# Banded attention with a ratio MLP: the attention's split matmuls replaced by plain float32 in quarter and half tiles of the array

## The chip, the cores and the metric

One core of one Trainium2 chip. The time is device microseconds of one execution. Before: 1083.75 us, median of 3 runs (1083.62 to 1083.78).

## The reference

Eight sequences of 576 positions, eight heads of 64. Each query sees the 128 keys up to its own; the result goes through an MLP whose activation is a ratio of polynomials.

```python
scores = scale * np.matmul(q, k.transpose(0, 1, 3, 2))
mask = (rel >= 0) & (rel < 128)
scores = np.where(mask, scores + bias[None], -1000000000.0)
attn = softmax(scores)                       # with 1e-9 in the denominator
x = (attn @ v).transpose(0, 2, 1, 3).reshape(B * S, H * D)    # 4608 x 512
h = x @ w_in                                 # 4608 x 2048
g = (a0 + a1 h + a2 h^2 + a3 h^3) / (1 + |b0| |h| + |b1| h^2 + 1e-6)
out = g @ w_out                              # 4608 x 512
```

All inputs and the output are float32.

## The kernel before

The 4608 tokens are 36 blocks of 128. The MLP takes them in 17 tiles t: 3 blocks, then 15 times 2, then 3 (`MLP`, L32). Attention works in units: a pair p of heads (128 rows: two heads of 64) and one or two blocks j (`TILES`, L30). A block of queries needs its own block of keys and the one before, 256 keys; a block at which a sequence begins (`kinds` 1) needs its own alone. While the MLP of tile t runs, the units of tile t + 1 are worked off.

For matmuls the kernel has two ways. In tile 0 operands are plain float32. From tile 1 on each operand is split into a high part of type float32r and the rest, and a product is three float32r matmuls: high by high, high by low, low by high. The weights are split once (`split`, L562), the keys, queries and values at every load.

A unit of `attention` (L400), with the lines that the change touches:

- `job` (L354) loads kqv into one buffer `kqv_raw`, ACT casts keys with queries and values to the high part (L389), DVE subtracts for the low part (L390).
- `scores` (L427): for each block and each of the three products, one matmul per head with 64 rows, 128 query columns as weights and 256 keys streaming (L433); head 0 is in rows 0 to 63, head 1 in rows 64 to 127, each with its own accumulator sc0, sc1.
- L447 copies, under the mask id_sb, the scores of the block before over those of the own block where a key lies ahead of its query, so that each query keeps 128 scores. L453 adds the bias and takes the top, L458 (ACT) the exponential with its sum, L466 to L468 the normalization.
- L477 transposes the probabilities on PE into pt; ACT (L480) and DVE (L482) make the high and low part p_all.
- POOL selects (L488, L489) the part that belongs to the own keys into p_own and leaves the rest in p_all, both with high and low.
- `values` (L495): for each block, own keys and then keys before, three matmuls of 128 rows, 128 value columns (both heads) and 256 streaming columns (both heads' probabilities, L500). Of the result px only the two diagonal head parts are used. Each of these up to four groups is a step of its own.
- ACT (L516) copies px into x_hi and DVE (L518) subtracts for x_lo, once per head over 64 partitions.

The MLP's matmuls are L599 (up, into h) and L655 (down, into acc), with the activation between on ACT, DVE and POOL. In tile 0 the weights arrive as 64-bit floats seen as two 32-bit words and are converted on POOL, ACT and DVE (`convert`, L529).

The order of everything is made ahead by a planner (`Plan`, L76): each step has a due time, engines and an estimated cost; the planner walks through time, gives each engine the earliest due step whose inputs and buffers are ready, and the instructions are written in that order, one fixed queue per engine. The constants at L265 to L271 are due times and offsets. Nothing is reordered at run time except by waits.

Of the kernel before, what the change touches and what calls it, by code (L numbers as in the profile page):

```python
# [20 lines left out]
P = 128  # L21
# [231 lines left out]
def banded_attention_ratio_mlp(ctx: ExitStack, tc: tile.TileContext, kqv, w_in, w_out, ab, bias, ident, out):  # L253
    nc = tc.nc
    const = ctx.enter_context(tc.tile_pool(name="const", bufs=1))
    sb3 = ctx.enter_context(tc.tile_pool(name="sb3", bufs=3))
# [3 lines left out]
    count = {id(const): 1, id(ps1): 1, id(sb2): 2, id(sb3): 3, id(ps3): 3}  # L260
    eng = {"p": nc.tensor, "a": nc.scalar, "v": nc.vector, "g": nc.gpsimd, "s": nc.sync}
    NTILE = len(MLP)


    A0, DA, T0, L0, L1 = -3.5, 1.542, 22.056, 90.639, 24.589  # L265
    AOFF, D2, D3, JL, VL = -0.627, 3.694, 6.675, 9.175, 4.671
    SP, SV, SA, SG = 0.204, 0.035, 0.013, 0.218
    LL = -1.886
    ML, ZA, ME, OE = 23.116, 0.956, 0.92, 12.957
    C0, DC, CO, DO, WL = 2.237, 6.361, 21.961, 5.327, 5.885  # L270
    S0, DS, SL, AW, BL = 120.646, 2.26, 6.993, 24.311, 4.541  # L271
# [82 lines left out]
    def job(u):  # L354
# [8 lines left out]
        if t == 0 and j == 0:  # L363
            plan.op(u0 - JL, {"s": 364}, lambda e: eng[e].dma_start(ap(first_kq)[:, p], src[:, P : 3 * P]), writes=[(first_kq, p)])
            plan.op(u0 - JL + VL, {"s": 182}, lambda e: eng[e].dma_start(ap(first_v)[:, p], src[:, 4 * P :]), writes=[(first_v, p)])
            kt = lambda part, b0, b1: ap(first_kq)[:, p, (b0 - 1) * P : (b1 - 1) * P]
            qt = lambda part, i: ap(first_kq)[:, p, P : 2 * P]
            vt = lambda part, b: ap(first_v)[:, p]
            return kt, qt, vt, 1, [(first_kq, p)], [(first_v, p)]
        if t == 0:  # L370
            tag = "hi" if p % 2 == 0 else "lo"
            kq = slot(sb2, [P, KMAX + QMAX], F32, "kq_32", tag="kq_" + tag)
            v = slot(sb2, [P, KMAX], F32, "v_32", tag="v_" + tag)
            plan.op(u0 - JL, {"s": 728 * 5 / 4}, lambda e: eng[e].dma_start(ap(kq), src[:, : W - ks]), writes=[(kq, 0)])
            plan.op(u0 - JL + VL, {"s": 546}, lambda e: eng[e].dma_start(ap(v), src[:, W - ks :]), writes=[(v, 0)])
            kt = lambda part, b0, b1: ap(kq)[:, b0 * P : b1 * P]
            qt = lambda part, i: ap(kq)[:, ks + i * P : ks + (i + 1) * P]
            vt = lambda part, b: ap(v)[:, b * P : (b + 1) * P]
            return kt, qt, vt, 1, [(kq, 0)], [(v, 0)]
        kq_hi = slot(sb2, [P, KMAX + QMAX], F32R, "kq_hi")  # L380
        kq_lo = slot(sb2, [P, KMAX + QMAX], F32R, "kq_lo")
        v_hi = slot(sb2, [P, KMAX], F32R, "v_hi")
        v_lo = slot(sb2, [P, KMAX], F32R, "v_lo")
        raw = slot(const, [P, WMAX], F32, "kqv_raw", tag="raw")
        plan.op(u0 - JL, {"s": 2002 * W / 1408}, lambda e: eng[e].dma_start(ap(raw)[:, :W], src), writes=[(raw, 0), (raw, 1)], after=1000 * (u0 - AW))
        for n, (c0, c1) in enumerate(((0, W - ks), (W - ks, W))):
            hi, lo = (kq_hi, kq_lo) if n == 0 else (v_hi, v_lo)
            N = c1 - c0
            plan.op(u0 - 4 + 2 * n, {"a": act(N, 0)}, lambda e, hi=hi, N=N, c0=c0, c1=c1: nc.scalar.copy(ap(hi)[:, :N], ap(raw)[:, c0:c1]), reads=[(raw, n)], writes=[(hi, 0)])  # L389
            plan.op(u0 - 3 + 2 * n, {"v": dve(N)}, lambda e, hi=hi, lo=lo, N=N, c0=c0, c1=c1: nc.vector.tensor_tensor(ap(lo)[:, :N], ap(raw)[:, c0:c1], ap(hi)[:, :N].bitcast(F32), ALU.subtract),  # L390
                    reads=[(raw, n), (hi, 0)], writes=[(lo, 0)], sb=True)
        kt = lambda part, b0, b1: ap((kq_hi, kq_lo)[part])[:, b0 * P : b1 * P]
        qt = lambda part, i: ap((kq_hi, kq_lo)[part])[:, ks + i * P : ks + (i + 1) * P]
        vt = lambda part, b: ap((v_hi, v_lo)[part])[:, b * P : (b + 1) * P]
        return kt, qt, vt, 2, [(kq_hi, 0), (kq_lo, 0)], [(v_hi, 0), (v_lo, 0)]
# [4 lines left out]
    def attention(u):  # L400
# [3 lines left out]
        kt, qt, vt, parts, kq_keys, v_keys = job(u)  # L404
# [14 lines left out]
        if t == 0 and u % 2:  # L419
            sc = [slot(ps1, [P, 2, 2, P], F32, f"sc{h}", tag=f"acc{h}") for h in range(2)]  # L420
        else:
            sc = [slot(ps1, [P, 2, 2, P], F32, f"sc{h}", tag=f"sc{h}") for h in range(2)]
# [4 lines left out]
        def scores(e, i):  # L427
            seq = ((0, 0), (0, 1), (1, 0)) if parts == 2 else ((0, 0),)
            b0 = i + own_only[i]
            for n, (x, y) in enumerate(seq):  # L430
                for h in range(2):
                    r = slice(64 * h, 64 * h + 64)
                    nc.tensor.matmul(ap(sc[h])[:, i, own_only[i] :], qt(x, i)[r], kt(y, b0, i + 2)[r], start=(n == 0), stop=(n == len(seq) - 1))  # L433

        def all_scores(e):
            for i in range(m):
                scores(e, i)

        o1 = plan.op(A, {"p": 187 + 354 * m if parts == 2 else sum(430 if x else 860 for x in own_only)}, all_scores, reads=kq_keys, writes=[(sc[0], 0), (sc[1], 0)], rows=0.5)
# [30 lines left out]

        pt = slot(ps1, [P, 4 * P], F32, "pt", tag="ptx")
        dt = F32R if parts == 2 else F32
        w = slot(sb2, [P, parts, 4 * P], dt, "p_all")

        def transpose(e):
            for y in range(n):
                nc.tensor.transpose(ap(pt)[:, y * P : (y + 1) * P], ap(pr)[:, y, :], ap(id_sb)[:, 0])  # L477

        o2 = plan.op(A + D2, {"p": 28 + 108 * n}, transpose, reads=[(pr, y) for y in range(n)] + [(id_sb, 0)], writes=[(pt, 0)])
        plan.op(A + D2 + 0.2, {"a": act(n * P, 1)}, lambda e: nc.scalar.copy(ap(w)[:, 0, : n * P], ap(pt)[:, : n * P]), reads=[(pt, 0)], writes=[(w, 0)])  # L480
        if parts == 2:
            plan.op(A + D2 + 0.3, {"v": dve(n * P)}, lambda e: nc.vector.tensor_sub(ap(w)[:, 1, : n * P], ap(pt)[:, : n * P], ap(w)[:, 0, : n * P].bitcast(F32)), reads=[(pt, 0), (w, 0)], writes=[(w, 1)])  # L482
        own = w
        if blocks:
            own = slot(const, [P, parts, 4 * P], dt, "p_own")
            pick = lambda y: ap(y)[:, :, : n * P].rearrange("p a (y q) -> p a y q", q=P)
            cost = {"g": 135 + 0.93 * parts * n * P}
            plan.op(A + D2 + 0.5, cost, lambda e: nc.gpsimd.affine_select(out=pick(own), in_=pick(w), pattern=[[0, parts], [0, n], [1, P]], compare_op=ALU.is_ge, fill=0.0, base=0, channel_multiplier=-1), reads=[(w, 0), (w, 1)], writes=[(own, 0), (own, 1)])  # L488
            plan.op(A + D2 + 0.6, cost, lambda e: nc.gpsimd.affine_select(out=pick(w), in_=pick(w), pattern=[[0, parts], [0, n], [-1, P]], compare_op=ALU.is_ge, fill=0.0, base=-1, channel_multiplier=1), reads=[(w, 0), (w, 1)], writes=[(w, 0), (w, 1)])  # L489
        if t not in xs:  # L490
            xs[t] = [slot(sb2, [P, NKC, P * MLP[t]], F32 if t == 0 else F32R, "x_hi"), slot(const, [P, NKC, P * MLP[t]], F32R, "x_lo", tag=f"x_lo{t % 2}") if t else None]
        xh, xl = xs[t]
        px = slot(ps3, [P, 4 * P], F32, "px", tag="h") if t == 0 else slot(ps1, [P, 4 * P], F32, "px", tag="ptx")

        def values(e, i, half, first, last):  # L495
            y = own if half else w
            c = slice(2 * i * P, 2 * (i + 1) * P)
            seq = ((0, 0), (0, 1), (1, 0)) if parts == 2 else ((0, 0),)
# [260 lines left out]
```

## Time and profile before

| | |
|---|---|
| median of 3 runs | 1083.75 us |
| the profiled execution | 1083.98 us, span 1082.2 us |
| DVE_READ and ACT reads of accumulators (L453, L458) | 23.7 and 54.3 us |
| DMA read and written | 58.07 MB and 9.44 MB, 62 GB/s over the span |

Read first the busy shares, then the stages: the attention of tile 0 and the load and conversion of the weights fill the first 120 us, splitting the weights the time to about 240 us, and from there every MLP tile of two blocks repeats with four attention units in it. A row of the table of stages has the stretch, its length, the busy time of PE, of its weight loads (PEld), DVE, ACT and POOL, each with a count of instructions, then PE's granted clock, the DMA engines' busy share and GB/s. PE's matmuls overlap in the records, so the time that one occupies PE is read from start to start.

### The profile page before, as it was taken

Reading aid. Unit: us, or ns where it says so; the run is one execution under the profiler, and the core shown is the slowest. Engines: PE = TensorE matmul, PEld = TensorE weight load, DVE = VectorE, ACT = ScalarE, POOL = GpSimd, SP = SyncE. Lnnn points to the kernel's source line nnn. Section 1 sums busy time; section 2 is a strip of 40 time slices with the busy share of each in tenths; the row PEclk is TensorE's granted clock in tenths of the full one; section 3 lists DMA queues with packets and bytes.
Section 4 is the critical chain, followed back from the end, with each engine's and each line's share of the span. In section 5 each row is a group of like instructions: output and inputs, shape, how many; then the busy total and the mean of one; then the engine's idle time right before and its main releaser. Section 6 shows DMA issues by size and latency. Waiting matters only on the chain.

```text
span 1082.2 us, 19767 instructions
## 1 busy us (share of the span) xinstructions
PE 1053.0 (97%) x6827; PEld 902.0 (83%) x6827; DVE 948.6 (88%) x2190; ACT 774.1 (72%) x1786; POOL 589.3 (54%) x581
## 2 busy tenths in 40 slices
PE   6899899999999999999999999999999999999998
PEld 4555468899889898989899989989899989888897
DVE  5899899998989898989988889989898989899776
ACT  6766778776767686867776777777676767677664
POOL 3745489854555464546455545555454545546442
PEclk9999999999999999999999999999999999999999
DMA  9625511020201111111111020111110202011000
GB/s 306 202 76 164 151 61 40 26 78 25 79 25 63 46 65 44 60 43 65 42 37 62 28 82 28 63 39 60 44 65 20 80 30 76 21 59 39 20 1 30
DMA packets 35477, 68.79 MB, mean 64 GB/s; under 512 B 3376, under 2 KB 19632, under 8 KB 35376
## 3 DMA queue, kind: packets, MB, share of 16 engines
q1 hardware_dynamic: 35376, 67.52, 19.1%
q8 instruction: 54, 0.88, 0.3%
q14 instruction: 47, 0.39, 0.1%
HBM read 58.07 MB, written 9.44 MB: 62 GB/s over the span
## 4 chain that ended last, share of the span: by engine, by line
PE 82%; DVE 7%; POOL 3%; ACT 3%; DMA 2%; issue 2%; SPq 0%; DVEq 0%; ACTq 0%; POOLq 0%
PE h L599 34%; PE acc L655 33%; PE px L500 8%; PE sc L433 5%; PE pt L477 2%; DMA raw_w<-in_w_out 1%; POOL pr L468 1%; DVE h L632 1%; POOL w_lo L574 1%; DVE g_p L626 1%; ACT pr L458 1%; DVE cv L558 1%; DVE g_p L627 1%; DVE v_lo L390 1%; DVE w L559 1%
## 5 line engine op out<-in xcount | busy, mean ns | idle before, releaser
L599 PE MATMUL h<-x_hi,wi_hi 128*128 128x256 f32 (+1 forms) x1024 | 302.5, 295 | 1.2 <-DVE g_l L640 1.2
L599 PE MATMUL h<-x_lo,wi_hi 128*128 128x256 f32 (+1 forms) x1024 | 291.0, 284 | 0.0
L623 POOL TENSOR_SCALAR g_q<-g_u,babs 128x512 f32<-128x512 f32 (+1 forms) x152 | 116.3, 765 | 307.6 <-ACT g_u L622 292.5
L599 PE MATMUL h<-x_hi,w_lo 128*128 128x256 f32 (+1 forms) x960 | 274.0, 285 | 1.5 <-DVE w_lo L574 1.5
L599 PEld LDWEIGHTS h<-x_lo,wi_hi 128*128 128x128 f32 x1024 | 192.5, 188 | 31.9 <-issue 0.7
L599 PEld LDWEIGHTS h<-x_hi,wi_hi 128*128 128x128 f32 x1024 | 192.6, 188 | 28.2 <-DVE g_l L640 1.8
L655 PE MATMUL acc<-wo_hi,g_h 128*128 128x512 f32 x528 | 209.0, 396 | 0.0
L625 POOL TENSOR_TENSOR g_q<-g_q,g_u 128x512 f32<-128x512 f32 (+1 forms) x152 | 191.0, 1257 | 8.9
L655 PE MATMUL acc<-w_lo,g_h 128*128 128x512 f32 x495 | 194.7, 393 | 0.0
L655 PE MATMUL acc<-wo_hi,g_l 128*128 128x512 f32 x528 | 194.3, 394 | 0.3 <-DVE g_l L640 0.3
L599 PEld LDWEIGHTS h<-x_hi,w_lo 128*128 128x128 f32 x960 | 180.6, 188 | 2.4 <-DVE w_lo L574 1.7
L622 ACT ACTIVATE g_u<-h 128x512 f32<-128x512 f32 (+1 forms) x152 | 87.0, 572 | 101.5 <-PE h L599 99.5
L628 ACT ACTIVATE g_u<-g_q,guard 128x512 f32<-128x512 f32 (+1 forms) x152 | 106.5, 701 | 50.3 <-POOL g_q L625 49.5
L488 POOL TENSOR_SCALAR_AFFINE_SELECT p_own<-p_all 128x1024 fp32r<-128x1024 f32 (+1 forms) x72 | 78.1, 1085 | 89.3 <-DVE p_all L482 88.7
L626 DVE TENSOR_TENSOR g_p<-h,g_p 128x512 f32<-128x512 f32 (+1 forms) x152 | 100.3, 660 | 29.9 <-ACT g_p L624 28.4
L458 ACT ACTIVATE pr<-pr,st 128x128 f32<-128x128 f32 x288 | 112.6, 392 | 18.2 <-DVE st L453 17.4
L631 DVE SCALAR_TENSOR_TENSOR g_q<-g_q,h 128x512 f32<-128x512 f32 (+1 forms) x152 | 99.6, 655 | 29.1 <-ACT h L630 25.4
L624 ACT ACTIVATE g_p<-h,na 128x512 f32<-128x512 f32 (+1 forms) x152 | 114.6, 754 | 0.5 <-DVE h L632 0.2
L640 DVE TENSOR_TENSOR g_l<-h,g_h 128x512 fp32r<-128x512 f32 (+1 forms) x136 | 90.9, 669 | 24.3 <-ACT g_h L639 23.4
L632 DVE SCALAR_TENSOR_TENSOR h<-g_p,na,h 128x512 f32<-128x512 f32 (+1 forms) x152 | 109.5, 720 | 0.1
L627 DVE SCALAR_TENSOR_TENSOR g_p<-g_p,na,h 128x512 f32<-128x512 f32 (+1 forms) x152 | 108.2, 712 | 0.6
L639 ACT CAST g_h<-h 128x512 fp32r<-128x512 f32 (+1 forms) x136 | 77.8, 572 | 40.7 <-DVE h L638 40.3
(91 smaller groups left out, 2257.5 us busy)
## 6 DMA issues: line engine op xcount, KB each, us to landing
kqv_raw<-in_kqv SPq DMA_DIRECT2D x64, 512.0 KB, 3.4
out<-o SPq DMA_DIRECT2D x33, 256.0 KB, 2.4
raw_w<-in_w_in SPq DMA_DIRECT2D x16, 512.0 KB, 4.4
raw_w<-in_w_out SPq DMA_DIRECT2D x16, 512.0 KB, 4.7
bias_t<-in_bias SPq DMA_DIRECT2D x44, 64.0 KB, 1.8
kq<-in_kqv SPq DMA_DIRECT2D x4, 320.0 KB, 5.6
kqv_raw<-in_kqv SPq DMA_DIRECT2D x4, 320.0 KB, 3.5
v<-in_kqv SPq DMA_DIRECT2D x4, 192.0 KB, 5.9
```

What stands on the lines that cost most here:

```text
L458: nc.scalar.activation(ap(pr)[:, y, :], ap(pr)[:, y, :], AF.Exp, bias=ap(st)[:, y : y + 1], scale=-1.0, accum_out=ap(st)[:, 4 + y : 5 + y])
L599: nc.tensor.matmul(h(n), w[:, k, :], x[:, k, :], start=(k == 0 and m == 0), stop=(k == NKC - 1 and m == len(seq) - 1))
L623: plan.op(E, {"g": tsc}, lambda e: nc.gpsimd.tensor_scalar(v(g_q), v(g_u), ap(babs)[:, 1:2], ap(babs)[:, 0:1], ALU.mult, ALU.add), reads=[ ...
L624: plan.op(E, {"a": act(W, 1, 2) - 20}, lambda e: nc.scalar.activation(v(g_p), v(h_s), AF.Identity, bias=ap(na)[:, 2:3], scale=ap(na)[:, 3: ...
L625: plan.op(E, {"g": ttc}, lambda e: nc.gpsimd.tensor_tensor(v(g_q), v(g_q), v(g_u), ALU.mult), reads=[(g_q, 0), (g_u, 0)], writes=[(g_q, 0)])
L626: plan.op(E, {"v": dve(W)}, lambda e: nc.vector.tensor_tensor(v(g_p), v(h_s), v(g_p), ALU.mult), reads=[(h_s, 0), (g_p, 0)], writes=[(g_p, ...
L627: plan.op(E, {"v": dve(W, 1)}, lambda e: stt(v(g_p), v(g_p), ap(na)[:, 1:2], v(h_s), ALU.add, ALU.mult), reads=[(h_s, 0), (g_p, 0)], write ...
L628: plan.op(E, {"a": act(W, 0, 1)}, lambda e: nc.scalar.activation(v(g_u), v(g_q), AF.Ln, bias=guard, scale=1.0), reads=[(g_q, 0)], writes=[ ...
L631: plan.op(E, {"v": dve(W)}, lambda e: stt(v(g_q), v(g_q), GUARD, v(h_s), ALU.add, ALU.mult), reads=[(g_q, 0), (h_s, 0)], writes=[(g_q, 0)])
L632: plan.op(E, {"v": dve(W, 1)}, lambda e: stt(v(h_s), v(g_p), ap(na)[:, 0:1], v(h_s), ALU.add, ALU.mult), reads=[(g_p, 0), (h_s, 0)], write ...
L640: plan.op(E, {"v": dve(W)}, lambda e: nc.vector.tensor_tensor(v(g_l), v(h_s), v(g_h).bitcast(F32), ALU.subtract), reads=[(h_s, 0), (g_h, 0 ...
L655: nc.tensor.matmul(ap(accs[t][i]), x[:, sl], w, start=(c == 0 and part == 0 and m == 0), stop=(c == NFC - 1 and (part == 1 or t == 0) and ...
```

## The change

From tile 1 on the attention's operands aren't split any more: every unit works in plain float32, as tile 0 did. The MLP keeps its split.

- The load is two DMAs, keys with queries and values, each into four buffers; the casts and subtractions of L389 and L390 go.
- Scores: the queries of a block are taken in two halves of 64, and a half sees only the 192 keys it can need. A matmul has 64 rows, 64 weight columns and 64, 128 or 192 streaming columns, at one of four places: head 0 or 1 by rows, half 0 or 1 by columns. The accumulators hold 192 scores per query instead of 256. For the first half, the keys are two matmuls, since their places in the accumulator are not adjacent.
- The predicated copy follows that layout, and a quarter of the mask in id_sb is zeroed at the start, on DVE.
- The low part of the probabilities (L482) goes; the selections on POOL are half as large. The layout of p_all is by head, then block and side.
- Values: each head has its own matmul with 64 weight columns at column 0 or 64, over that head's probabilities alone, so both heads' results lie where they are used. A block of keys that two blocks of queries share streams once, 256 columns. All of it is one step.
- px is copied to x_hi once over 128 partitions, and subtracted once for x_lo.
- The planner's constants and some costs are set anew.

```diff
-    SP, SV, SA, SG = 0.204, 0.035, 0.013, 0.218
+    SP, SV, SA, SG = 0.204, 0.035, 0.013, 0.16
...
+        plan.op(-7, {"v": 100}, lambda e: nc.vector.memset(ap(id_sb)[:Q, 1, Q:], 0.0), reads=[(id_sb, 0)], writes=[(id_sb, 0)])
...
-        for n, (c0, c1) in enumerate(((0, W - ks), (W - ks, W))):
...
+        kq = slot(sb4, [P, KMAX + QMAX], F32, "kq")
+        v = slot(sb4, [P, KMAX], F32, "v")
...
+        def scores(e):
             for i in range(m):
+                for half in range(2):
+                    q = slice(Q * half, Q * half + Q)
+                    own = (i + 1) * P
+                    if own_only[i]:
+                        todo = [(slice(Q, 3 * Q), own, own + P)]
+                    elif half:
+                        todo = [(slice(0, 3 * Q), own - Q, own + P)]
+                    else:
+                        todo = [(slice(0, 3 * Q, 2), own - P, own), (slice(Q, 2 * Q), own, own + Q)]
+                    for dst, k0, k1 in todo:
+                        for h in range(2):
+                            r = slice(64 * h, 64 * h + 64)
...
+                            nc.tensor.matmul(to, qt(i)[r, q], kt(k0, k1)[r], start=True, stop=True, tile_position=(64 * h, Q * half))
...
-        if parts == 2:
-            plan.op(A + D2 + 0.3, {"v": dve(n * P)}, lambda e: nc.vector.tensor_sub(ap(w)[:, 1, : n * P], ap(pt)[:, : n * P], ap(w)[:, 0, : n * P].bitcast(F32)), reads=[(pt, 0), (w, 0)], writes=[(w, 1)])
...
+        def values(e):
+            for n, (b, i0, i1) in enumerate(runs):
...
+                for h in range(2):
+                    r = slice(64 * h, 64 * h + 64)
+                    nc.tensor.matmul(ap(px)[r, i0:i1], vt(b)[:, r], ap(w)[:, h, c0 : c0 + i1 - i0], start=new, stop=done, tile_position=(0, 64 * h))
```

In `values`, `runs` are the blocks of keys b with the blocks of queries i0 to i1 that see them; the shared block comes first.

More of the change, by code (lines that the diff above doesn't have):

```diff
@@ L380, in job @@
[L380 to L385, printed above, removed]
-        for n, (c0, c1) in enumerate(((0, W - ks), (W - ks, W))):
[L387 to L395, printed above, removed]
+            kt = lambda c0, c1: ap(first_kq)[:, p, c0 - P : c1 - P]
+            qt = lambda i: ap(first_kq)[:, p, P : 2 * P]
+            vt = lambda b: ap(first_v)[:, p]
+            return kt, qt, vt, [(first_kq, p)], [(first_v, p)]
@@ L419, in attention @@
         if t == 0 and u % 2:
-            sc = [slot(ps1, [P, 2, 2, P], F32, f"sc{h}", tag=f"acc{h}") for h in range(2)]
+            sc = [slot(ps1, [P, 2, 3 * Q], F32, f"sc{h}", tag=f"acc{h}") for h in range(2)]
         else:
-            sc = [slot(ps1, [P, 2, 2, P], F32, f"sc{h}", tag=f"sc{h}") for h in range(2)]
+            sc = [slot(ps1, [P, 2, 3 * Q], F32, f"sc{h}", tag=f"sc{h}") for h in range(2)]
         pr = slot(sb3, [P, 4, P], F32, "pr")
@@ L471, in attention @@
         pt = slot(ps1, [P, 4 * P], F32, "pt", tag="ptx")
-        dt = F32R if parts == 2 else F32
-        w = slot(sb2, [P, parts, 4 * P], dt, "p_all")
+        w = slot(sb2, [P, 2, 4, P], F32, "p_all")
+        base = 0 if blocks else 1
         def transpose(e):
-            for y in range(n):
-                nc.tensor.transpose(ap(pt)[:, y * P : (y + 1) * P], ap(pr)[:, y, :], ap(id_sb)[:, 0])
+            for h in range(2):
+                for i in range(m):
+                    nc.tensor.transpose(ap(pt)[:, (m * h + i) * P : (m * h + i + 1) * P], ap(pr)[:, 2 * i + h, :], ap(id_sb)[:, 0])
@@ L483, in attention @@
-        own = w
+        plan.op(A + D2 + 0.2, {"a": act(n * P, 1)}, lambda e: nc.scalar.copy(side(base), ap(pt)[:, : n * P].rearrange("q (h i c) -> q h i c", h=2, i=m)), reads=[(pt, 0)], writes=[(w, base)])
         if blocks:
[L485 to L489, printed above, removed]
+            cost = {"g": 135 + 0.93 * n * P}
+            for k, sign in ((1, 1), (0, -1)):
+                plan.op(A + D2 + 0.6 - 0.1 * k, cost, lambda e, k=k, sign=sign: nc.gpsimd.affine_select(out=side(k), in_=side(0), pattern=[[0, 2], [0, m], [sign, P]], compare_op=ALU.is_ge, fill=0.0, base=k - 1, channel_multiplier=-sign), reads=[(w, 0)], writes=[(w, k)])
@@ L490, in attention @@
         if t not in xs:
-            xs[t] = [slot(sb2, [P, NKC, P * MLP[t]], F32 if t == 0 else F32R, "x_hi"), slot(const, [P, NKC, P * MLP[t]], F32R, "x_lo", tag=f"x_lo{t % 2}") if t else None]
+            xs[t] = [slot(const, [P, NKC, P * MLP[t]], F32 if t == 0 else F32R, "x_hi", tag=f"x_hi{t % 2}"), slot(const, [P, NKC, P * MLP[t]], F32R, "x_lo", tag=f"x_lo{t % 2}") if t else None]
+        px = slot(ps3, [P, 2, P], F32, "px", tag="h") if t == 0 else slot(ps1, [P, 2, P], F32, "px", tag="ptx")
@@ L492, in attention @@
         xh, xl = xs[t]
[L493 to L498, printed above, removed]
-            for k, (a, b) in enumerate(seq):
-                nc.tensor.matmul(ap(px)[:, c], vt(a, i + half), ap(y)[:, b, c], start=(first and k == 0), stop=(last and k == len(seq) - 1))
@@ L502, in attention @@
-        for i in range(m):
-            halves = [1] if kinds[i] == 1 else [1, 0]
-            for k, half in enumerate(halves):
-                o3 = plan.op(A + D3, {"p": 357 if parts == 2 else 430}, lambda e, i=i, half=half, k=k, halves=halves: values(e, i, half, k == 0, k == len(halves) - 1),
-                        reads=v_keys + [(own if half else w, 0), (own if half else w, 1)], writes=[(px, 0)])
+        runs = []
+        for b in range(m + 1):
+            ends = [i for i, half in ((b - 1, 1), (b, 0)) if 0 <= i < m and (half or kinds[i] != 1)]
+            if ends:
+                runs.append((b, ends[0], ends[-1] + 1))
@@ new lines, in attention @@
+        runs.sort(key=lambda r: r[1] - r[2])
+        full = runs[0][2] - runs[0][1] == m
+        if not full:
+            runs.sort()
+        def values(e):
+            for n, (b, i0, i1) in enumerate(runs):
+                new = n == 0 if full else n == 0 or i0 >= runs[n - 1][2]
+                done = n == len(runs) - 1 or not full and runs[n + 1][1] >= i1
+                c0 = 2 * b - 1 if i0 == b - 1 else 2 * b
+                for h in range(2):
+                    r = slice(64 * h, 64 * h + 64)
+                    nc.tensor.matmul(ap(px)[r, i0:i1], vt(b)[:, r], ap(w)[:, h, c0 : c0 + i1 - i0], start=new, stop=done, tile_position=(0, 64 * h))
@@ L507, in attention @@
+        o3 = plan.op(A + D3, {"p": 187 + sum(215 * (i1 - i0) for b, i0, i1 in runs)}, values, reads=v_keys + [(w, 0), (w, 1)], writes=[(px, 0)], rows=0.5)
         stage[u] = (o1, o2, o3)
```

76 lines of the change are left out of this document (32 added, 44 removed).

## The prediction

> **What bounds the kernel now.** First the page's totals, the 40 slices and the chain that ended last; then the table by stages.
>
> ```profile
> span 1082.2 us, 19767 instructions
> ...
> PE 1053.0 (97%) x6827; PEld 902.0 (83%) x6827; DVE 948.6 (88%) x2190; ACT 774.1 (72%) x1786; POOL 589.3 (54%) x581
> PE   6899899999999999999999999999999999999998
> ...
> PE 82%; DVE 7%; POOL 3%; ACT 3%; DMA 2%; issue 2%; SPq 0%; DVEq 0%; ACTq 0%; POOLq 0%
> ```
> ```profile
> 22.00:55.00 33.00, 27.64 (x122) 18.01 (x123) 26.64 (x79) 24.56 (x69) 25.35 (x34) 0.90 0.66 224
> 55.00:120.00 65.00, 61.97 (x215) 33.35 (x214) 60.36 (x130) 42.91 (x90) 32.07 (x38) 1.00 0.41 127
> 120.00:180.00 60.00, 53.30 (x292) 37.99 (x293) 55.28 (x118) 48.77 (x112) 46.87 (x43) 1.00 0.23 75
> 180.00:240.00 60.00, 58.60 (x406) 51.93 (x405) 58.57 (x126) 46.48 (x106) 45.76 (x39) 1.00 0.15 47
> 300.00:1000.00 700.00, 699.08 (x4909) 629.35 (x4907) 625.84 (x1453) 507.03 (x1171) 370.60 (x351) 1.00 0.15 50
> ```
>
> The columns are length, then busy time of PE, PEld, DVE, ACT, POOL, then clock and DMA. From 300 us on PE lacks 0.92 us of 700, at full clock: there a microsecond of PE stream removed is a microsecond of time, and DVE, ACT or POOL work is worth nothing. From 22 to 240 us PE lacks 5.36 + 3.03 + 6.70 + 1.40 = 16.5 us while DVE is busy 200.85 of 218: there, and only there, a lighter DVE can pay.
>
> **The change on PE.** What a unit (two query blocks, one pair of heads) streams now:
>
> ```profile
> 308.83 0.39 PE L655 MATMUL acc<-wo_hi,g_l 128*128 128x512 f32 x1
> 309.15 0.39 PE L433 MATMUL sc<-kq_hi 64*128 64x256 f32 x2
> 309.38 0.28 PE L433 MATMUL sc<-kq_lo,kq_hi 64*128 64x256 f32 x2
> ...
> 309.84 0.28 PE L433 MATMUL sc<-kq_hi,kq_lo 64*128 64x256 f32 x2
> 310.05 0.39 PE L599 MATMUL h<-x_hi,wi_hi 128*128 128x256 f32 x1
> 310.27 0.28 PE L599 MATMUL h<-x_lo,wi_hi 128*128 128x256 f32 x1
> ```
> ```profile
> 303.24 0.36 PE px L500 x3
> 303.59 0.36 PE h L599 x3
> ```
>
> Matmuls overlap, so I count from start to start. A 256-column split pass takes 0.117 us (303.24 to 303.59 is three); in the scores the two heads run side by side at nearly that pace (309.38 to 309.84 is four). Scores: 6 passes, 0.70 us. Around them, the 512-column pass of 308.83 should have ended twice 0.117 later, at 309.065, and the next normal pass of 310.05 should have started 0.118 ahead of its successor, at 310.152: between lie 1.09 us, so **0.385 us go into changing to half-array tiles and back**. Values: one group of three passes is 0.354 us, and a plain unit has four (two blocks, each with its own keys and the ones before): 1.416 us.
>
> What plain float32 streams:
>
> ```profile
> 30.94 0.59 PE L500 MATMUL px<-p_own,v 128*128 128x256 f32 x2
> 31.38 0.59 PE L500 MATMUL px<-p_all,v 128*128 128x256 f32 x2
> ```
> ```profile
> 14.68 1.13 PE L433 MATMUL sc<-kq 64*128 64x256 f32 x8
> 15.75 0.70 PE L500 MATMUL px<-p_all,v_first 128*128 128x256 f32 x2
> ```
> ```profile
> 14.38 0.38 PE L500 MATMUL px<-p_all,v_first 128*128 128x256 f32 x1
> 14.68 0.49 PE L433 MATMUL sc<-kq 64*128 64x256 f32 x2
> ```
>
> One float32 matmul leaves two records; at 256 columns they take 0.43 us together, 0.216 each. Eight in half-array tiles took 1.07 us; eight in a row would take 1.73, four pairs 0.86 with the rest for the change of tiles. The last fence is the view cut off at 14.75: both heads' first passes are under way, while a single one lasts to about 15.17. So float32 passes of two row halves do run at once, and the second head did not wait for the first head's second pass.
>
> Whether two **column** halves run at once no row shows. Between full overlap and none I take full, for the nearest row is that of row halves. Then a block's scores are 192 columns in each of four quarters, two passes: 2 x 0.216 x 192/256 = 0.324 us, 0.65 a unit against 0.70. Values are 256 + 128 + 128 columns in each column half, two passes: 4 x 0.216 = 0.864 against 1.416. But the values now need a change of tiles of their own, which they had not; between nothing and twice the scores' price (26 us less or more over 68 units) I take the 0.385 shown. A plain unit goes from 0.70 + 0.385 + 1.416 = 2.50 to 0.65 + 0.385 + 0.864 + 0.385 = 2.28: 0.22 less. After the first tile there are 68 units: 52 plain (11.4 us less), 12 that hold a block with own keys only (scores 0.55 to 0.54, values of three groups 1.06 to 0.65: with the changes of tiles 2.00 to 1.96, 0.5 less) and 4 of one block (half the passes, 1.44 to 1.53, 0.3 more). **Minus 11.6 us**, all on the path.
>
> One part of the 0.385 depends on the weight load ahead of the first pass: 310.27 - 310.05 - 0.118 = 0.10 us where a kind of tile begins.
>
> ```profile
> 509.04 0.22 PE L433 MATMUL sc<-kq_hi 64*128 64x128 f32 x2
> 509.10 0.27 PE L433 MATMUL sc<-kq_lo,kq_hi 64*128 64x128 f32 x2
> 509.21 0.28 PE L433 MATMUL sc<-kq_hi,kq_lo 64*128 64x128 f32 x2
> ```
>
> A 128-column pass should take half of 0.117; from 509.10 to 509.21 it took 0.11, held by loading 128 weight columns, so 0.10 is that load. The new tiles load 64 columns, which no row shows. Between nothing and 0.10 at each of the two entries into them I keep 0.10, the row; the other end is 68 x 0.2 = 14 us less, and goes into the range. The Trainium skill (TensorE: Matmul & The Clock Gate, LDWEIGHTS) says that a load's time goes with its columns, whatever its rows; by it half of those 14 us would go, an estimate of 7, and the sum would be 1057.
>
> **The change on the other engines.**
>
> ```profile
> L489 POOL TENSOR_SCALAR_AFFINE_SELECT p_all<-p_all 128x1024 fp32r<-128x1024 f32 x64 | 75.0, 1173 | 3.8
> ...
> L390 DVE TENSOR_TENSOR kq_lo<-kqv_raw,kq_hi 128x640 fp32r<-128x640 f32 x64 | 59.9, 936 | 5.3 <-ACT kq_hi L389 5.0
> ...
> L518 DVE TENSOR_TENSOR x_lo<-px,x_hi 64x256 fp32r<-64x256 f32 x128 | 53.8, 420 | 6.9 <-ACT x_hi L516 5.4
> ...
> L482 DVE TENSOR_TENSOR p_all<-pt,p_all 128x512 fp32r<-128x512 f32 x64 | 43.8, 684 | 2.3 <-ACT p_all L480 2.2
> ...
> L390 DVE TENSOR_TENSOR v_lo<-kqv_raw,v_hi 128x384 fp32r<-128x384 f32 x64 | 42.3, 661 | 0.7
> ...
> L488 POOL TENSOR_SCALAR_AFFINE_SELECT p_own<-p_all 128x512 f32<-128x512 f32 x4 | 2.5, 636 | 0.3 <-PE px L500 0.3
> ```
>
> Per unit DVE loses 0.936 + 0.661 + 0.684 and one of two 0.420 (one instruction over 128 partitions instead of two over 64; I price it by its columns): 2.70 us. ACT loses its two casts of keys, queries and values and one of two of the result; of POOL's two selections each falls from 1.173 (or its like on L488) to 0.636. After 240 us that is worth nothing. Before it, the 8 units of tiles 1 and 2 free 21.6 us of DVE, more than PE's missing 16.5. Not all comes back: weights still arrive and are converted one buffer at a time. Between 0 and 16.5 I take half, **minus 8 us**.
>
> Priced at nothing: the zeroing of a quarter of id_sb (DVE, at the start; DVE is waiting for the first loads then; uncovered it delays the first transpose by some tenths), the strided predicated copy (same 256 elements a head), the second DMA issue per unit on SP (DMA is 15% busy; with four buffers instead of one a load waits less for its slot, so outputs and weights behind it on SP do too), and the values in one step. That step now waits for both selections and holds the MLP matmuls behind it on PE; in the steady stage PE waited for nothing, and POOL, 53% busy, finishes earlier.
>
> The profiled execution took 1083.98 us, 1.8 more than its span and 0.2 more than the median 1083.75. Sum: 1083.98 - 11.6 - 8 = 1064.4, at the median **1064**.
>
> **Rivals.**
>
> *Column halves of one row group share a queue* (slower). If a tile's pass cannot start before the pass ahead of it in program order in the same rows has started, h0's second pass holds back h1's first. Passes of 64, 128, 192 and 256 columns last 0.054, 0.108, 0.162 and 0.216. Scores in one row half: the first query half's 128 columns end at 0.216, its 64 at 0.324; the second half's first pass starts with the last of these, at 0.270, its second at 0.432, and only then the next block: two blocks 2 x 0.432 + 0.162 = 1.03 instead of 0.65. Values: h1's first pass starts with h0's second, so the 256 columns take 0.648 and each 128 another 0.216: 1.08 instead of 0.864. 0.6 more a unit, +0.38 against before. Over 52 plain units 19.5, over the others 7, less the front's 8: +19, **1102 us**. It decides from 0.29 us lost per unit, (11.6 + 8)/68. For it: nothing here shows column halves. Against: two row halves did not hold each other up, though each matmul is two passes.
>
> *All passes start in program order*, row halves too. Then second passes start at 0.108, 0.216, 0.270, 0.378, 0.540 and 0.702, where the next block begins, and the last ends at 0.864: 1.57 a unit for scores, 1.08 for values, +0.91 on plain units: 47 + 14 - 8 = +53, **1137 us**. Against it stands the view cut off at 14.75, unless the program interleaves the two heads' passes. The Trainium skill (TensorE: Matmul & The Clock Gate, The mechanism) says that matmuls start and end strictly in program order, which is this rival. That view speaks against it for row halves, and no row tells for column halves.
>
> *Column halves don't overlap at all*: the change doesn't do what it says. Scores 1.30, values 1.73 a unit, 1.3 more than before on plain ones: 67 + 17 - 8 = +76, **1160 us**.
>
> *The saving is given back*: changing tiles for values costs 0.67, within its bounds, instead of 0.385; 68 x 0.29 = 19.6 us: **1084 us**. For it: values need whole-height column tiles, a kind the trace lacks. Against: nothing makes it dearer than the scores' change.
>
> **How the numbers follow.** Forecast 0.62, with its own range 1042 (8 more from the front, 14 from shorter loads) to 1072 (nothing from the front); shared queue 0.20; program order 0.04; no overlap 0.08; given back 0.06, of which 0.04 within 0.2% and the rest split. What a measurement can tell from no change is about 0.2%, 2.2 us. Faster 0.63, within 0.04, slower 0.33. The range takes in the shared queue and leaves out program order, no overlap and the ends of several bounds taken together: 1044 to 1103.
>
> **What would show it.** In the timeline of the changed kernel: four score records of a block starting within some 10 ns of each other, and the next MLP matmul about 1.0 us after a unit's first score; values pairs starting together and about 1.1 us in all. Starts of the second column half after the first half's second pass mean the shared queue. PE still at 99% from 300 us on; DVE there from 89% to about 70%; PE's missing time between 22 and 240 us at about 8. Wrong I would be if PE shows waits on POOL's selections in the steady stage, or if the front doesn't move.

## The result, and the profile after

The changed kernel takes 1052.8 us (median of 4 runs, 1051.87 to 1054.29) against 1083.68 us before in the same session: ratio 0.9719, 95% interval 0.9702 to 0.9736. That is 30.9 us less, inside the range, 11 us below the forecast.

The page of the changed kernel: totals, PE's 40 slices, and the chain that ended last by engine.

```profile
span 1051.1 us, 21072 instructions
...
PE 1028.2 (98%) x7687; PEld 855.4 (81%) x7687; DVE 775.8 (74%) x1923; ACT 666.2 (63%) x1574; POOL 508.7 (48%) x577
PE   6899999999999999999999999999999999999998
...
PE 88%; DVE 3%; DMA 3%; POOL 2%; ACT 2%; issue 1%; SPq 1%; DVEq 0%; POOLq 0%; ACTq 0%
```

The table of stages of the changed kernel, same columns as before (length; PE, PEld, DVE, ACT, POOL busy; clock, DMA share, GB/s).

```profile
22.00:55.00 33.00, 26.64 (x220) 18.39 (x221) 23.04 (x80) 22.25 (x69) 23.91 (x34) 0.87 0.71 238
55.00:120.00 65.00, 63.51 (x272) 33.60 (x271) 58.25 (x133) 43.81 (x95) 34.39 (x46) 1.00 0.44 142
120.00:180.00 60.00, 56.90 (x395) 41.41 (x394) 53.67 (x119) 47.05 (x109) 47.97 (x45) 1.00 0.28 92
180.00:240.00 60.00, 60.00 (x476) 52.34 (x475) 46.28 (x102) 39.67 (x86) 31.98 (x35) 1.00 0.14 43
300.00:1000.00 700.00, 700.00 (x5523) 608.73 (x5518) 508.28 (x1263) 438.05 (x1035) 323.15 (x362) 1.00 0.16 48
```

PE is the bound as before, and now without a gap from 300 to 1000 us. DVE's share there fell from 89% to 508.28 / 700 = 73%, and nothing came of that: the steady stage is still PE's stream. From 22 to 240 us PE lacks 6.36 + 1.49 + 3.10 + 0 = 10.95 us; it was 16.5.

**A unit's scores and values now.** The timeline of the changed kernel, PE alone, around one unit's scores:

```profile
403.82 0.40 PE L657 MATMUL acc<-wo_hi,g_l 128*128 128x512 f32 x1
404.15 0.94 PE L430 MATMUL sc<-kq 64*64 64x128 f32 x24
405.02 0.39 PE L601 MATMUL h<-x_hi,wi_hi 128*128 128x256 f32 x1
405.24 0.28 PE L601 MATMUL h<-x_lo,wi_hi 128*128 128x256 f32 x1
```

and around one unit's values:

```profile
395.81 0.28 PE L601 MATMUL h<-x_hi,w_lo 128*128 128x256 f32 x1
396.01 1.09 PE L507 MATMUL px<-p_all,v 128*64 128x256 f32 x12
397.03 0.38 PE L601 MATMUL h<-x_hi,wi_hi 128*128 128x256 f32 x1
397.26 0.28 PE L601 MATMUL h<-x_lo,wi_hi 128*128 128x256 f32 x1
```

Counted as in the prediction, from where the pass ahead should have ended to where the next MLP pass would have started at its normal pace: scores 403.82 + 0.235 = 404.055 to 405.24 - 0.118 = 405.122, **1.07 us** (1.09 before, 1.035 forecast). Values 395.81 + 0.118 = 395.928 to 397.26 - 0.118 = 397.142, **1.21 us** (1.42 before, 1.25 forecast).

**Do column halves run at once?** The same timeline cut off at 404.16 and at 404.19:

```profile
404.15 0.33 PE L430 MATMUL sc<-kq 64*64 64x128 f32 x2
```
```profile
404.15 0.41 PE L430 MATMUL sc<-kq 64*64 64x128 f32 x4
```

By 404.19 the first passes of all four places have started: two of the first query half at 404.149 and 404.156, two of the second at 404.176 and 404.182. The first half's second passes start only at 404.309. So a second column half waits neither for the first half's second pass (shared queue, program order) nor for its end (no overlap): three rivals fall with these two rows. The passes that start at 404.176 are the 192-column ones, which the program writes behind the first half's 64-column ones, and those start at 404.418. So the statement ahead of the prediction that nothing is reordered at run time holds for the planner's steps, and not for matmuls at different places of the array. The values' pairs, which lie in the two column halves, start 6 to 7 ns apart (the first at 396.015 and 396.021).

The second passes of the first half start 0.160 us after its first ones, while 128 columns last 0.108: 0.05 us of entry, where before it was 0.107 (309.379 - 309.155 - 0.117, in the unit that the prediction shows). The loads of weights, by the view of one line (minimum, median and maximum ns), first before, for 128 weight columns, then after, for 64:

```profile
L433 PEld LDWEIGHTS sc<-kq x32: 182/186/187, 12.3 to 24.3; 64*128 64x128 f32 x32
```
```profile
L430 PEld LDWEIGHTS sc<-kq x24: 129/133/135, 404.1 to 404.8; 64*64 64x64 f32 x24
```

Half the columns, 53 ns less, about as much as the entry lost (55). The Trainium skill (TensorE: Matmul & The Clock Gate, LDWEIGHTS) lets a load's time go with its columns; these rows agree with it.

**Where the 31 us went.** I cut the time where the last copy of MLP tile 3's result starts. Up to there both versions have done the same MLP matmuls and the same units, and so they have behind it. The first mark is in ACT's timeline, before and after (the first row holds two copies, the second some 0.5 us behind the first: 340.1):

```profile
339.61 1.07 ACT L683 COPY o<-acc 128x512 f32<-128x512 f32 x2
```
```profile
322.69 0.62 ACT L685 COPY o<-acc 128x512 f32<-128x512 f32 x1
```

The other end is the last copy of all, in DVE's timeline, before and after:

```profile
1078.43 0.42 DVE L680 COPY o<-acc 128x256 f32<-128x256 f32 x1 [0.25 <-ACT o L680]
```
```profile
1047.41 0.42 DVE L682 COPY o<-acc 128x256 f32<-128x256 f32 x1 [0.25 <-ACT o L682]
```

So 31.0 us are 17.4 in the **front** (340.1 to 322.7) and 13.6 in the **rest** (738.3 to 724.7).

In the rest every PE record can be counted from start to start. The MLP passes at their normal pace come to 599.0 us in both kernels. With the rows below that makes 737.2 and 723.4 us, 1.1 and 1.3 less than the rest, which runs from copy to copy and not from pass to pass:

| rest, us on PE | before | after |
|---|---|---|
| scores of 48 units with their changes of tiles | 51.3 | 48.6 |
| values of 50 units with their changes of tiles | 66.6 | 57.2 |
| transposes, short stalls and all else | 20.3 | 18.6 |

Attention's own bursts give 12.1 of the 13.8. The last line's 1.7 are, but for rounding, stalls that the kernel before had and the one after lacks: four stretched MLP passes (1.0 us) and 0.9 us ahead of transposes.

### The profile page after: what moved, and what is told of

Same layout as the page of the kernel before. It is cut to its first block, busy times and chain, and to the rows that moved or that the text cites. A ratio compares the mean times of both kernels' runs of the same rounds, so it can differ in the third digit from the quotient of the medians.

```text
span 1051.1 us, 21072 instructions
## 1 busy us (share of the span) xinstructions
PE 1028.2 (98%) x7687; PEld 855.4 (81%) x7687; DVE 775.8 (74%) x1923; ACT 666.2 (63%) x1574; POOL 508.7 (48%) x577
## 4 chain that ended last, share of the span: by engine, by line
PE 88%; DVE 3%; DMA 3%; POOL 2%; ACT 2%; issue 1%; SPq 1%; DVEq 0%; POOLq 0%; ACTq 0%
PE h L601 38%; PE acc L657 37%; PE px L507 6%; PE sc L430 5%; PE pt L474 3%; DMA raw_w<-in_w_out 1%; DMA raw_w<-in_w_in 1%; DMA ab_sb<-in_ab 1%; ACT pr L453 1%; POOL w_lo L576 1%; POOL g_q L627 0%; DVE w L561 0%; POOL g_q L625 0%; DVE cv L560 0%; DVE g_q L633 0%
## 5 line engine op out<-in xcount | busy, mean ns | idle before, releaser
L601 PE MATMUL h<-x_hi,wi_hi 128*128 128x256 f32 (+1 forms) x1024 | 307.0, 300 | 0.0
L627 POOL TENSOR_TENSOR g_q<-g_q,g_u 128x512 f32<-128x512 f32 (+1 forms) x152 | 188.6, 1241 | 8.4
L453 ACT ACTIVATE pr<-pr,st 128x128 f32<-128x128 f32 x288 | 112.6, 393 | 32.3 <-DVE st L448 32.1
L482 POOL TENSOR_SCALAR_AFFINE_SELECT p_all<-p_all 128x512 f32<-128x512 f32 (+1 forms) x144 | 91.0, 633 | 62.2 <-ACT p_all L478 58.3
L463 POOL TENSOR_TENSOR pr<-pr,st 128x512 f32<-128x512 f32 (+1 forms) x76 | 76.6, 1008 | 60.3 <-DVE st L462 34.2
```

Source lines behind the costliest of these rows:

```text
L453: nc.scalar.activation(ap(pr)[:, y, :], ap(pr)[:, y, :], AF.Exp, bias=ap(st)[:, y : y + 1], scale=-1.0, accum_out=ap(st)[:, 4 + y : 5 + y])
L601: nc.tensor.matmul(h(n), w[:, k, :], x[:, k, :], start=(k == 0 and m == 0), stop=(k == NKC - 1 and m == len(seq) - 1))
L627: plan.op(E, {"g": ttc}, lambda e: nc.gpsimd.tensor_tensor(v(g_q), v(g_q), v(g_u), ALU.mult), reads=[(g_q, 0), (g_u, 0)], writes=[(g_q, 0)])
```

## The experiments

All times are medians, ratios are to the kernel before on the same chip. "Front" ends with the last copy of tile 3, "rest" runs to the last copy of all, "PE lacks" is 300 us less PE's busy time in the first 300 us. "Half clock" is the part of that busy time in which the trace grants TensorE half its clock.

| kernel | us | ratio, 95% interval | front | rest | PE lacks | half clock |
|---|---|---|---|---|---|---|
| before | 1083.7 | | 340.1 | 738.3 | 24.1 | 6.8 |
| after | 1052.8 | 0.9719 (0.9702 to 0.9736) | 322.7 | 724.7 | 18.8 | 12.3 |
| e1_old_constants | 1062.7 | 0.9804 (0.979 to 0.9819) | 332.2 | 724.3 | 25.9 | 20.9 |
| e2_dve_back | 1077.8 | 0.9938 (0.9922 to 0.9954) | 349.0 | 724.4 | 38.3 | 25.8 |
| e9_dve_order_only | 1071.0 | 0.9888 (0.9873 to 0.9903) | 342.4 | 724.4 | 32.3 | 25.7 |
| e3_two_buffers | 1063.9 | 0.9809 (0.9793 to 0.9826) | 334.5 | 724.4 | 26.1 | 23.7 |
| e5_scores_as_before | 1076.7 | 0.9927 (0.9912 to 0.9942) | 345.4 | 726.1 | 30.4 | 27.5 |
| e4_values_full | 1102.3 | 1.0166 (1.0146 to 1.0186) | 346.4 | 746.4 | 28.5 | 14.5 |
| e8_dve_load_only | 1149.4 | 1.061 (1.0594 to 1.0625) | 355.2 | 789.6 | 38.1 | 23.5 |
| e10_before_new_constants | 1113.8 | 1.028 (1.0254 to 1.0305) | 352.8 | 753.3 | 30.4 | 20.5 |
| e6_fused | 1069.5 | 0.988 (0.9861 to 0.99) | 340.5 | 723.7 | 29.4 | 30.7 |
| e11_fused_middle | 1043.8 | 0.9634 (0.9619 to 0.9648) | 318.9 | 719.2 | 18.0 | 12.4 |
| e12_fused_to_15 | 1042.8 | 0.963 (0.9613 to 0.9647) | 319.2 | 718.4 | 18.6 | 11.8 |

Read down the column of the rest: of the kernels that keep the new values, it stays within 2 us of 724.5, however they fare in the front, until scores and values are fused or extra DVE work is put into a fixed order.

The last column belongs to the front as much as the one before it. In one such stretch of e1 the record of the window is

```profile
143.90:150.70 6.80, 5.21 (x18) 4.21 (x19) 6.24 (x21) 5.06 (x15) 6.65 (x7) 0.50 0.01 2
```

(clock 0.50), and there a 256-column MLP pass starts 0.213 us after the one ahead of it instead of 0.117. PE counts as busy, but does little more than half the work. So what a worse order costs PE is, as an estimate, the rise in what PE lacks and half of the rise in this column. For e9 against the change that is 13.5 + 6.7 = 20.2 us, and its front is 19.7 longer; for e3 7.3 + 5.7 = 13.0 against 11.8; for e1 7.1 + 4.3 = 11.4 against 9.5.

### The planner's constants (e1_old_constants, e10_before_new_constants)

The change with the constants of the kernel before, and the kernel before with those of the change:

```diff
-    AOFF, D2, D3, JL, VL = -0.627, 3.708, 6.675, 9.175, 4.671
-    SP, SV, SA, SG = 0.204, 0.035, 0.013, 0.16
-    LL = 5.242
-    ML, ZA, ME, OE = 23.116, 0.956, -1.043, 9.586
+    AOFF, D2, D3, JL, VL = -0.627, 3.694, 6.675, 9.175, 4.671
+    SP, SV, SA, SG = 0.204, 0.035, 0.013, 0.218
+    LL = -1.886
+    ML, ZA, ME, OE = 23.116, 0.956, 0.92, 12.957
...
```

> The changed kernel with the planner's constants of the kernel before. Theory (the front gains because DVE is lighter): 1052.8 becomes 1053 to 1056, tile 0 of the MLP still ends near 152 us. Rival (the new due times made the front's gain): 8 to 13 us come back, 1061 to 1066, and tile 0 ends near 158 us. From 300 us on both expect the same 54.9 us a tile.

> The kernel before with the changed kernel's planner constants. Theory (each set of constants is fitted to its own kernel's costs, so the constants' 10 us belong to the change only together with the new costs): no gain, 1084 to 1094. Rival (the new constants are better in themselves): 1074 or less.

Without new constants the change gives 1062.7 us, so they are worth 9.9 us, and all of it in the front. ACT's timeline of e1:

```profile
332.20 0.62 ACT L685 COPY o<-acc 128x512 f32<-128x512 f32 x1
```

The first 300 us as one window, before, after and e1:

```profile
0.00:300.00 300.00, 275.95 (x1530) 203.23 (x1531) 263.54 (x626) 220.03 (x522) 187.68 (x193) 0.99 0.34 109
```
```profile
0.00:300.00 300.00, 281.23 (x1944) 205.08 (x1948) 232.39 (x593) 200.66 (x486) 168.78 (x196) 0.97 0.35 114
```
```profile
0.00:300.00 300.00, 274.08 (x1851) 199.07 (x1852) 228.00 (x577) 195.65 (x470) 163.70 (x191) 0.95 0.35 113
```

With the old constants PE lacks 300 - 274.08 = 25.9 us, not less than the 24.1 before, although DVE is 35.5 us less busy. The front of e1 is 7.9 us shorter all the same: the matmuls to be done in it are shorter (14 plain and 4 own-key units, and tile 0's units, whose values streamed full columns). Counted from start to next start, at most a record's length, the values hold PE for 42.6 us of the front before and 25.4 in e1; the scores for 25.3 and 25.8, the MLP for 233.1 and 237.6, more of it at half clock. The new order then takes 7.1 us out of PE's missing time, and 8.6 us of PE's time at half clock go. So the expectation's rival came true in the total, not its theory; tile 0 ends at 162.6, later than either said. (The 54.9 us a tile that this and later expectations name is the length of one tile; from tile 3 to 14 the pace is 55.7 in the change and 55.6 in e1.)

The constants are no gain by themselves: under the kernel before, they cost 30 us (in the profiled execution 12.7 in the front and 15.0 in the rest). I had expected at most 10. They fit one kernel's costs, and are part of this change, not an addition to it.

### DVE's old work put back (e2_dve_back, e9_dve_order_only, e8_dve_load_only)

e2 gives each unit four DVE instructions that write to a scratch tile, as long together as the work that the change removed (2.7 us), and lets the planner place them; e9 plans the same steps, so that every queue has the same order, and issues nothing in them; e8 keeps the order of the changed kernel and puts the extra instructions in front of the predicated copies (its expectation says behind) and behind the subtraction for x_lo, unknown to the planner.

```diff
+        if t:
+            for n, (x, N) in enumerate(((kq, W - ks), (v, ks))):
+                plan.op(u0 - 3 + 2 * n, {"v": dve(N)}, lambda e, x=x, N=N: nc.vector.tensor_tensor(ap(scr)[:, :N], ap(x)[:, :N], ap(x)[:, :N], ALU.subtract), reads=[(x, 0)], writes=[(scr, 0)], sb=True)
...
+            plan.op(A + D2 + 0.3, {"v": dve(n * P)}, lambda e: nc.vector.tensor_tensor(ap(spare_out)[:, : n * P], ap(pt)[:, : n * P], ap(pr)[:, :n].rearrange("p y c -> p (y c)"), ALU.subtract), reads=[(pt, 0)] + [(pr, y) for y in range(n)], writes=[(spare_out, 0)])
...
+            plan.op(A + D3 + 0.4, {"v": dve(m * P)}, lambda e: nc.vector.tensor_sub(ap(spare_out)[:, : m * P], src(), into(xh).bitcast(F32)), reads=[(px, 0), (xh, (p, j))], writes=[(spare_out, 0)])
```
```diff
+        def with_extra(h):
+            if t:
+                busy(640 if h else 384)
...
+        def sub_twice():
+            nc.vector.tensor_sub(into(xl), src(), into(xh).bitcast(F32))
+            busy(512)
+            busy(256)
```

> The changed kernel with the DVE work of the old one put back per unit from tile 1 on: four instructions of the old sizes, 2.7 us, into a scratch tile that nobody reads. Theory (lighter DVE makes the front's gain): 8 to 13 us come back, 1061 to 1066, all of it before 270 us, and the pace of 54.9 us a tile after that stays within 0.2. Rival (new due times or deeper buffers made it): under 3 us.

> The order that the planner made for the run with the DVE work put back, with those four instructions a unit left out: the order of e2 without its load. Theory 1 (load): most of the 25 us is gone, under 1061. Theory 2 (order): 15 us or more stay, 1068 or later, because the steps are laid out around work that isn't there.

> The changed kernel with the order of every queue kept, and the old DVE work (2.7 us a unit from tile 1 on) added as instructions on a scratch tile, unknown to the planner, behind the predicated copies and the low part of x. Theory 1 (DVE's load sets the front): 8 us or more back, 1061 or later, before 270 us. Theory 2 (the order laid out for the kernel sets the front): under 4 us. Both expect the pace after 300 us unchanged.

e2 lost 25 us, more than any theory gave it. e9, with the same order and no extra work, shows why: 18.2 of the 25 come with the order alone, and 6.8 with the load, so e9's second theory held. Tile 3's end in ACT's timeline, e9 and e2 (each row two copies):

```profile
341.96 1.10 ACT L696 COPY o<-acc 128x512 f32<-128x512 f32 x2
```
```profile
348.57 1.10 ACT L696 COPY o<-acc 128x512 f32<-128x512 f32 x2
```

and the first 300 us, e9 and e2:

```profile
0.00:300.00 300.00, 267.73 (x1784) 190.62 (x1784) 220.75 (x562) 190.31 (x461) 160.04 (x187) 0.94 0.34 110
```
```profile
0.00:300.00 300.00, 261.71 (x1738) 185.63 (x1739) 249.06 (x606) 185.23 (x446) 157.32 (x182) 0.95 0.34 110
```

In one and the same order, 28.3 us more of DVE work take 6.0 us from PE, and the front ends 6.6 us later. In the rest, both take 724.4 us. The stage from 300 to 1000 us, e2 and e8:

```profile
300.00:1000.00 700.00, 700.00 (x5589) 604.35 (x5588) 615.02 (x1486) 440.26 (x1041) 338.54 (x363) 1.00 0.16 49
```
```profile
300.00:1000.00 700.00, 656.27 (x5117) 562.24 (x5117) 610.30 (x1331) 403.87 (x946) 322.93 (x325) 1.00 0.15 46
```

Planned, 615 us of DVE hide completely under PE. Unplanned, 610 us cost PE 43.7 us of 700. PE's waits in e8, over the whole run (us in all, how often, the longest):

```profile
PE pt L487 <- POOL pr L476: 41.2, 40, 3.7
PE px L520 <- POOL p_all L495: 18.7, 23, 2.7
```

The extra instructions delay the predicated copies, these the exponentials and POOL's normalization, and a transpose that stands at a fixed place in PE's queue waits for it, with the MLP matmuls behind it. So e8 does not price the load that was removed; it prices a delay inside the unit's chain that the order was not laid out for. Both theories expected an unchanged pace after 300 us, and it went from 55.7 to 61.0 us a tile.

### Buffers for the loads (e3_two_buffers)

```diff
-        kq = slot(sb4, [P, KMAX + QMAX], F32, "kq")
-        v = slot(sb4, [P, KMAX], F32, "v")
+        kq = slot(sb2, [P, KMAX + QMAX], F32, "kq")
+        v = slot(sb2, [P, KMAX], F32, "v")
```

> The changed kernel with two buffers instead of four for the loads of keys, queries and values. Theory (lighter DVE): within 2 us of 1052.8. Rival (loads that wait less for a buffer made the front's gain): 6 us or more back, in the first 120 us.

It took 1063.9 us, 11 more, where I had expected no more than 2. All of it lies in the front (334.5 against 322.7); the rest is the same (724.4). Fewer buffers also give another order, so whether the front misses the buffers or only the order that the constants were fitted to is not told apart here.

### One half of the change at a time (e5_scores_as_before, e4_values_full)

e5 goes back to split scores in row halves, with the cast and the subtraction for keys and queries, and with two buffers instead of four for their load; the values stay new. e4 keeps the new scores and streams the values in plain float32 over all 128 weight columns, so that half of each result is not used; the result is copied and subtracted once per head again.

```diff
+            hi, lo = slot(sb2, [P, KMAX + QMAX], F32R, "kq_hi"), slot(sb2, [P, KMAX + QMAX], F32R, "kq_lo")
...
+                seq = ((0, 0), (0, 1), (1, 0)) if t else ((0, 0),)
+                for s, (x, y) in enumerate(seq):
+                    for h in range(2):
+                        r = slice(64 * h, 64 * h + 64)
+                        nc.tensor.matmul(ap(sc[h])[:, i, own_only[i] :], qt(x, i)[r], kt(y, (i + own_only[i]) * P, (i + 2) * P)[r], start=(s == 0), stop=(s == len(seq) - 1))
```
```diff
-                for h in range(2):
-                    r = slice(64 * h, 64 * h + 64)
-                    nc.tensor.matmul(ap(px)[r, i0:i1], vt(b)[:, r], ap(w)[:, h, c0 : c0 + i1 - i0], start=new, stop=done, tile_position=(0, 64 * h))
+                nc.tensor.matmul(ap(px)[:, :, i0:i1], vt(b), ap(w)[:, :, c0 : c0 + i1 - i0], start=new, stop=done)
```

> The changed kernel with the scores of the old one: keys and queries split on ACT and DVE, three float32r products in row halves. Theory (nearly all PE gain is in the values): 1.10 instead of 1.07 us a unit, 56 units, about 2 us, and a third of the DVE work is back, 3 to 4 us in the front: 1057 to 1059. Rival (quartered scores carry half of the gain): 1065 or more.

> The changed kernel with the values in plain float32 over all 128 weight columns: both heads' weights against both heads' probabilities, half of the result unused, no tiles. Theory (two column halves run at once and save half of the stream, less 0.385 us for changing tiles): 4 x 0.432 = 1.73 instead of 1.21 us in a plain unit, 1.30 instead of 1.03 in those with a block of own keys, so 30 us more: 1083, give or take 10 for another order in the front; pace 57.0 us a tile. Rival (column halves save nothing that counts): 1053, pace 54.9.

In e5 the rest is 1.4 us longer (726.1): quartered scores are worth little on PE. The other 22.7 us are lost in the front, to a new order, more time at half clock, and perhaps the two buffers, which in e3 went with 11.8 us of front. So the total is past the rival's 1065, but not for the rival's reason. In e4 one unit's values, from its PE timeline:

```profile
408.33 0.40 PE L657 MATMUL acc<-wo_hi,g_l 128*128 128x512 f32 x1
408.56 1.88 PE L505 MATMUL px<-p_all,v 128*128 128x512 f32 x6
410.09 0.58 PE L657 MATMUL acc<-wo_hi,g_h 128*128 128x512 f32 x1
410.51 0.39 PE L657 MATMUL acc<-w_lo,g_h 128*128 128x512 f32 x1
```

From 408.33 + 0.235 = 408.565 to 410.51 - 0.235 = 410.275 they take 1.71 us instead of 1.21, and the rest is 21.6 us longer. Plain float32 alone would have been slower than the split it replaces (1.42 before). What pays in the values is that the two heads' halves of the array work at once. e4's total missed the expectation (1083, 10 either way) because its front, too, is 23.7 us longer.

### Scores and values side by side (e6_fused, e11_fused_middle, e12_fused_to_15)

If changing the kind of tile is what costs, a unit's values directly followed by the next unit's scores should save one change. They become one step of the plan: e6 from tile 1 on, e11 only for the units of tiles 4 to 14, e12 to 15.

```diff
+            def both(e):
+                values(e)
+                if next_scores:
+                    next_scores(e)
+
+            o3 = plan.op(A + D3, {"p": 187 + sum(215 * (i1 - i0) for b, i0, i1 in runs) + cost_next}, both, reads=v_keys + [(w, 0), (w, 1)] + list(next_reads), writes=[(px, 0)] + list(next_writes), rows=0.5)
...
+        if not (4 <= t <= 14):
+            finish()
+        else:
+            pending[u] = finish
```

> The changed kernel with a unit's values and the next unit's scores issued as one step from tile 1 on, so that PE goes from full tiles to column halves, to quarters and back, instead of there and back twice. Theory (a change of tiles costs 0.19 us whichever way): one change fewer in some 62 units, 12 us: 1041, and 54.1 us a tile, give or take 10 for the front. Rival (each kind of tile costs its own 0.385): 1053 and 54.9.

> Values of a unit and scores of the next as one step, but only for the units of tiles 4 to 14, so that the queues in the front and at the end stay as they are in the changed kernel. Theory (the fused step saved 1.16 us a tile in e6, and what e6 lost lies in the front and in the last two tiles): 11 tiles, 12 to 13 us less than the changed kernel: 1040 to 1042. Rival (fusing delays a unit's own chain, and the loss appears wherever it ends): 1053 or more.

> As e11, with tile 15's units too. Theory: one tile more, 1039 to 1041. Rival (the end of e6 was lost by fusing close to the last tile): more than e11 by 3 us or more.

e6 takes 1069.5 us where the theory said 1041. A tile of four units got shorter by 1.16 us (54.57 against 55.73 from tile 3 to 14), but its front lost 17.8 us to the new order, and of the 11 x 1.16 = 12.8 us all but 1.0 was given back after tile 14 (rest 723.7): PE waits there, once for 5.2 us for ACT's g_h, and its clock is at half for 6.8 us from 999.0 on. e11 leaves the front's order as it is, and takes 1043.8 us, 9 less than the change. Its PE timeline:

```profile
445.30 0.39 PE L676 MATMUL acc<-w_lo,g_h 128*128 128x512 f32 x1
445.62 1.09 PE L512 MATMUL px<-p_all,v 128*64 128x256 f32 x12
446.64 0.94 PE L431 MATMUL sc<-kq 64*64 64x128 f32 x24
447.51 0.39 PE L620 MATMUL h<-x_hi,wi_hi 128*128 128x256 f32 x1
447.74 0.28 PE L620 MATMUL h<-x_lo,wi_hi 128*128 128x256 f32 x1
```

From 445.535 to 447.622 both take 2.09 us, against 1.07 + 1.21 = 2.28 apart: 0.20 us saved for a unit, and 44 units give 8.7 of the 9.1 us. The columns of front and rest can't be read by themselves here: the fused steps leave two units' scores and one unit's values, some 3 us of PE, behind the mark that in the change lie ahead of it, so the front is 3.8 us shorter and the rest only 5.5. I had expected 1040 to 1042, from e6's tiles; those had gained something else as well. e12 takes 1042.8 us, 10 below the change and 41 below the kernel before. That is the lowest median here, but its runs (1042.4 to 1045.3) and e11's (1043.5 to 1044.2) overlap, so one more fused tile isn't shown to gain, as the theory had it (1039 to 1041), and it loses nothing, against its rival.

## Why the prediction was right, and where its sizes were off

**The bound.** "From 300 us on ... DVE, ACT or POOL work is worth nothing": right, as long as the order is laid out for that work. e2 puts DVE's work back, and its rest is 724.4 us against 724.7; e8, where the planner doesn't know of it, loses 65 us there.

**Minus 11.6 us on PE.** The mechanism is right, and the four rivals are out: three by the starts of the quarter tiles, *the saving is given back* by the values' 1.21 us where it needed about 1.5. The term was too small. The rest holds 38 plain, 8 own-key and 4 single-block units, for which the prediction's own prices give 8.4 + 0.3 - 0.4 = 8.3 us. Measured: 12.1 from the bursts and 1.7 from stalls that went. In the mean of the rest's records, a plain unit's scores went from 1.10 to 1.07 and its four groups of values from 4 x 0.36 to 1.21: 0.26 less, not 0.22. The own-key units went from 1.06 + 3 x 0.36 to 0.93 + 1.00, about 0.2 less where 0.04 was forecast. For single-block units 0.09 more was forecast; they came out about 0.05 less in the mean, and about even without one stalled burst of the kernel before.

**The entry by the weight load.** I kept 0.10 us at each entry; the scores' is 0.05. Scores took 0.03 more than forecast all the same, values 0.04 less. So the Trainium skill's rule (TensorE: Matmul & The Clock Gate, LDWEIGHTS) was right for that piece. That the 1057 it gave lies nearer to the result is luck, for the 11 us that were missing have other sources, named below. The rest of the scores' burst streamed slower than the 0.65 I had put there: in the second block of a unit the 192-column pass holds its place 0.207 us (404.551 to 404.758) and not 0.162, and the second column half starts 0.027 late.

**Minus 8 us in the front, from DVE.** The size was right by accident. With the old constants the front gained 7.9 us, and PE lacked as much as before: the gain was PE's own shorter stream, above all the values', part of which I had already counted in the 11.6 and part of which (tile 0's values) I had not counted at all. That a lighter DVE helps in the front is shown by e2 against e9, 6.8 us in one and the same order, but in the order that the old constants lay out, PE's missing time shows nothing of it. My sign for this term, "PE's missing ~8 in 22 to 240", came out at 10.95, and only with the new constants (218 - 201.37 = 16.6 with the old).

**Nothing for the rest, and no word for the constants.** The copies, the memset and the second DMA issue show nowhere on the path, and the waits on POOL's selections are 2.7 us in all, none behind the front. The step that failed is the planner's constants, which stand in the diff and have no price in the sum. They are worth 9.9 us. Without them the change takes 1062.7 us against 1064 forecast, where 5.4 us too little in the rest and 3.4 too much in the front nearly cancel. With them it takes 1052.8.

**What stays open.** Every variant whose front was laid out anew with the changed kernel's constants ends it 12 to 26 us later, by gaps and by time at half clock together. How much of the front's 17.4 us is DVE's relief, how much the four buffers and how much a good fit of the order cannot be split into parts that add up: each experiment on one of them also changed the order. The record does show that the values' shorter stream is a large part: they hold PE for 42.6 us of the front before and 25.2 after.

## What to carry to other kernels

Count a matmul's cost from start to start with the change of tile kind on both sides, and put work of the same kind side by side: here each change costs some 0.2 us, and fusing saved 10 us without a single matmul less. Where an order is laid out ahead of time from costs, a change of costs without a new fit, or a fit without its change, misleads by more than the change itself (9.9 us less with it, 30 more without). So judge each experiment by stages, with a mark that lies at the same work in all versions, and where it doesn't, as in the fused ones, count what moved across it.

## What the runs showed that was not expected

- 2.7 us of DVE work per unit cost nothing behind the front where the planner knew of it (e2), and slowed that stage from 55.7 to 61.0 us per tile where it did not (e8), at a lower DVE load (610 against 615 us of 700). In a fixed order, slack in an engine's share says little about slack at a place.
- Plain float32 passes at four quarters of the array start within 33 ns (404.149 to 404.182). The second column half's lie 20 to 27 ns behind the first's; two heads in different row halves lie 6 to 7 ns apart.
- Half the weight columns shorten a load by 53 ns (186 to 133 ns in the median), and the entry into a tile by as much.
